# Retention and a gated feed-forward on one core: the output DMAs of seven of eight units move from SyncE's queue to GpSimd's

## The chip, the cores and the metric

The kernel runs on one core of one Trainium2 chip. The time is that of one execution on the device in microseconds (us). The engines are named as the profile names them: PE is TensorE (PEld its weight loads), DVE is VectorE, ACT is ScalarE, POOL is GpSimd, SP is SyncE; SPq and POOLq are the instruction queues of the last two, in which they issue DMAs and wait for semaphores.

## The reference

A linear attention with decay feeds a gated feed-forward with a three-tap convolution along the sequence. B, H, S, D = 4, 8, 768, 64; the model width is 512 and the inner width 1024.

```python
for t in range(S):
    state = gamma[None, :, None, None] * state + np.einsum('bhd,bhe->bhde', k[:, :, t], v[:, :, t])
    y[:, :, t] = scale * np.einsum('bhd,bhde->bhe', q[:, :, t], state)
...
h = np.maximum(x @ w_in, 0.0)
hp = np.concatenate([zeros, h, zeros], axis=1)
for k in range(K):
    conv_out += conv_w[k][None, None, :] * hp[:, k:k + S, :]
gate = 1.0 / (1.0 + np.exp(-conv_out))
return h * gate @ w_out
```

x is y with its heads side by side, so it has 4 x 768 rows of 512, and so has the result: 6.3 MB of float32.

## The kernel before

The sequence is cut into steps of 64 positions for two of the four batches: 24 steps. Each step loads q, k (both layouts) and v (L381, L385, L389, L393) into one of four `rw` buffers and makes scores, state and y (all PE work of L461, through the helper `multiply`). Three steps make a unit of 2 x 192 rows; there are eight units, 0 to 7. Of a unit, x is split into two parts of the same width by ACT (L537) and DVE (L542) and kept in one of three `xu` buffers. Then the feed-forward runs over eight pieces of the inner width: 12 matmuls of the first product into one of two PSUM banks (`ps_m`, L636), the relu by ACT which empties the bank (L643), the middle tap by ACT (L651), the outer taps by DVE (L656), and for each pair of pieces the gate by ACT (L661), its product by DVE (L666) and the split of the result by ACT and DVE (L670, L675). The second product (L688) adds up four pairs in a PSUM bank (`ps_yo`) for each tile of 128 rows, three tiles to a unit.

A finished tile is copied by ACT (`put`, L696) from PSUM into one of four staging buffers (`t2`, shared with the weights' preparation), and `out_` (L708) writes it to HBM. A unit has 192 rows of either batch, so its first and third tile are one DMA of 128 rows each, and the middle one is two of 64 rows: four DMAs for a unit. The last tile of the last unit is treated in two halves of 256 columns, which makes five DMAs for unit 7, and 33 in all.

The order of the work is written out by hand: `ORDER` has one string of letters for each of PE, DVE, ACT, POOL and the DMA queue. `plan` walks through them with estimated costs, gives every task its buffer (a staging buffer counts as free 2600 ns after its output is issued), and returns one list of tasks in the order of their estimated start. The kernel emits this list. Each engine runs its own instructions in the order of emission, and the tile framework adds the semaphore waits that the buffers need. The DMA string holds loads and outputs in one order, and both go to SP. The plan gives unit 2's three tiles one and the same staging buffer, so the copy of the second tile follows the output of the first, and that of the third the output of the second.

POOL has one kind of task, `x_tiles` (L526): a memset of the edge columns of a unit's `xu` buffer, which only units 0, 3, 4 and 7 have. In the emitted list that of unit 7 stands between the outputs of unit 2 and those of unit 3; the other three stand before the first output.

L779 is the end of the program: SP waits there for all that is open, and the engines drain and meet.

Of the kernel before, what the change touches and what calls it, by code (L numbers as in the profile page):

```python
# [18 lines left out]
P = 128  # L19
# [25 lines left out]
LAST = (len(UNITS) - 1, UNITS[-1] - 1)  # L45
# [240 lines left out]
def retention_then_gated_ffn(  # L286
# [10 lines left out]
    nc = tc.nc  # L297
# [379 lines left out]
    def columns(u, t, h):  # L677
        return slice(h * DM // 2, (h + 1) * DM // 2) if (u, t) == LAST else slice(0, DM)
# [11 lines left out]
    def put_tiles(u, t, h):  # L690
        cs = columns(u, t, h)
        return buf("t2", ("o", u, t, h))[:, : cs.stop - cs.start], buf("ps_yo", ("o", u, t, h))[:, : cs.stop - cs.start]
# [5 lines left out]
    @emits  # L698
    def out_(u, t, h):

        o, width = put_tiles(u, t, h)[0], UNITS[u] * C
        c0, tok = divmod(FIRST_STEP[u], NC)
        at = t * P
        while at < (t + 1) * P:
            b, i = divmod(at, width)
            n = min(width - i, (t + 1) * P - at)
            r0 = (c0 * G + b) * S + tok * C + i
            nc.sync.dma_start(out[r0 : r0 + n, columns(u, t, h)], o[at - t * P : at - t * P + n])  # L708
            at += n

    emit["out"] = out_
# [2 lines left out]
    for i in range(WARM_UP_SMALL):  # L714
        j, cross, at = i % 2, i // 2 % 2, i // 4 * D
# [67 lines left out]
```

## Time and profile before

| | us |
|---|---|
| runs of the kernel before | 353.55, 350.33, 352.9; median 352.9 |
| the profiled execution, its own time | 351.29 |
| its span, from the first to the last instruction | 348.9 |

PE is busy for 96% of the span, DVE for 64%, ACT for 54%, POOL for less than 1%. The granted clock of TensorE is 0.995 over the span. All DMAs that the program issues, 130 loads and 33 outputs, go through one queue; 34.0 MB are read and 6.3 MB written.

The time of a run is some 2.4 us longer than the span of the profile. Times in rows are us from the start of the span. In a timeline a row is: start, duration, engine, line, operation, written<-read tiles and shape, the count of instructions merged in the row, and in brackets the idle time of the engine before it and what ended that. For an output the profile calls the staging buffer `t` and the result `out_y`.

### The profile page before, as it was taken

How to read it: one execution, taken by the hardware profiler on the slowest of the kernel's cores; microseconds unless marked ns; L12 is line 12 of the kernel's file. 1: busy time of each engine (PE TensorE's matmuls, PEld its weight loads, DVE VectorE, ACT ScalarE, POOL GpSimd, SP SyncE). 2: the span in 40 equal slices, each digit the busy share in tenths (PEclk: the TensorE clock that was granted, in tenths of full speed). 3: DMA queues.
4: the chain of work that ended last, by engine and by line, in shares of the span. 5: the costliest groups of instructions: out<-in, count | busy, mean ns of one | idle time of the engine just before them, and what ended most of it. 6: DMA issues, size and time to landing. Idle time of an engine off the chain costs nothing.

```text
span 348.9 us, 9816 instructions
## 1 busy us (share of the span) xinstructions
PE 335.6 (96%) x4306; PEld 301.7 (86%) x4306; DVE 225.0 (64%) x370; ACT 187.4 (54%) x373; POOL 0.7 (0%) x8
## 2 busy tenths in 40 slices
PE   6879999899999999999999999999999999999996
PEld 5769999798898988988988888898889889999885
DVE  0879899979899978796666427065556242558160
ACT  1668798577675566656364345272555332545442
POOL 0000000000000000000000000000000000000000
PEclk9989999999999999999999999999999999999999
DMA  7989877958380033403003820200002001000203
GB/s 260 374 269 327 281 265 249 348 197 290 109 272 0 2 122 114 159 2 122 0 0 113 284 61 2 60 2 32 2 28 62 2 32 32 0 33 0 90 2 90
DMA packets 22491, 40.90 MB, mean 117 GB/s; under 512 B 2737, under 2 KB 2993, under 8 KB 22449
## 3 DMA queue, kind: packets, MB, share of 16 engines
q1 hardware_dynamic: 22448, 40.28, 34.4%
q8 instruction: 34, 0.56, 0.7%
q14 instruction: 9, 0.07, 0.1%
HBM read 33.98 MB, written 6.29 MB: 115 GB/s over the span
## 4 chain that ended last, share of the span: by engine, by line
PE 89%; DMA 8%; issue 1%; SPq 1%; ACT 0%
PE ps_m L636 38%; PE ps_yo L688 37%; PE ps_s L461 5%; PE ps_st L461 4%; PE ps_yo L461 4%; DMA out_y<-t 3%; DMA rw<-in_qk 3%; DMA rw<-in_kv 2%; PE ps_yo L373 1%; SPq L381 0%; ACT t L696 0%; SPq L393 0%; SPq L389 0%; SPq L385 0%; ACT hc L643 0%
## 5 line engine op out<-in xcount | busy, mean ns | idle before, releaser
L636 PE MATMUL ps_m<-xu,w 128*128 128x388 f32 x768 | 143.6, 340 | 1.0 <-ACT hc L643 1.0
L688 PE MATMUL ps_yo<-w,g 128*128 128x512 f32 (+1 forms) x600 | 140.4, 386 | 0.0
L636 PEld LDWEIGHTS ps_m<-xu,w 128*128 128x128 f32 x768 | 135.9, 188 | 4.7 <-ACT hc L643 1.4
L688 PEld LDWEIGHTS ps_yo<-w,g 128*128 128x128 f32 x600 | 108.6, 188 | 21.9
L656 DVE SCALAR_TENSOR_TENSOR hc<-hc,cw_sb,hc 128x384 f32<-128x384 f32 x128 | 74.5, 614 | 33.8 <-ACT hc L651 33.5
L643 ACT ACTIVATE hc<-ps_m 128x388 f32<-128x388 f32 x64 | 31.3, 491 | 44.5 <-PE ps_m L636 40.4
L461 PE MATMUL ps_yo<-rw 64*64 64x64 f32 (+1 forms) x1408 | 48.8, 225 | 3.1 <-issue 3.0
L461 PEld LDWEIGHTS ps_yo<-rw 64*64 64x64 f32 (+1 forms) x1408 | 45.4, 138 | 3.7 <-issue 3.3
L675 DVE TENSOR_TENSOR g<-hc,g 128x768 fp32r<-128x768 f32 x32 | 30.4, 956 | 24.6 <-ACT g L670 24.3
L666 DVE TENSOR_TENSOR hc<-hc,hc 128x768 f32<-128x768 f32 x32 | 30.3, 954 | 16.2 <-ACT hc L661 15.9
L670 ACT CAST g<-hc 128x768 fp32r<-128x768 f32 x32 | 26.5, 828 | 22.8 <-PE ps_yo L688 20.6
L651 ACT ACTIVATE hc<-hc,cw_sb 128x384 f32<-128x384 f32 x64 | 37.7, 611 | 1.4 <-DVE g L675 1.3
L661 ACT ACTIVATE hc<-hc 128x768 f32<-128x768 f32 x32 | 27.0, 846 | 16.6 <-DVE hc L656 16.5
L461 PEld LDWEIGHTS ps_s<-rw 64*64 64x64 f32 (+1 forms) x720 | 25.2, 139 | 10.4 <-issue 4.4
L461 PE MATMUL ps_s<-rw 64*64 64x64 f32 (+1 forms) x720 | 28.8, 227 | 4.0 <-DMA w<-in_w_in 2.5
L696 ACT COPY t<-ps_yo 128x512 f32<-128x512 f32 (+1 forms) x25 | 14.0, 567 | 27.0 <-PE ps_yo L688 22.3
L542 DVE TENSOR_TENSOR xu<-ps_yo,xu 128x512 fp32r<-128x512 f32 x24 | 16.5, 687 | 17.5 <-ACT xu L537 17.5
L461 PE MATMUL ps_st<-rw 64*64 64x64 f32 (+1 forms) x672 | 24.6, 222 | 0.7 <-issue 0.7
L461 PEld LDWEIGHTS ps_st<-rw 64*64 64x64 f32 (+1 forms) x672 | 22.5, 138 | 0.8 <-issue 0.8
L537 ACT CAST xu<-ps_yo 128x512 fp32r<-128x512 f32 x24 | 14.1, 592 | 13.4 <-PE ps_yo L461 12.1
L511 DVE TENSOR_TENSOR rw<-ps_s,const_sb 128x512 f32<-128x512 f32 x22 | 15.1, 686 | 8.0 <-PE ps_s L461 8.0
L519 ACT COPY rw<-ps_st 128x512 f32<-128x512 f32 x21 | 12.2, 582 | 12.8 <-PE ps_yo L461 12.7
(38 smaller groups left out, 144.4 us busy)
## 6 DMA issues: line engine op xcount, KB each, us to landing
rw<-in_qk SPq DMA_DIRECT2D x48, 256.0 KB, 4.6
rw<-in_kv SPq DMA_DIRECT2D x48, 256.0 KB, 5.1
w<-in_w_in SPq DMA_DIRECT2D x16, 256.0 KB, 5.2
w<-in_w_out SPq DMA_DIRECT2D x16, 256.0 KB, 5.0
out_y<-t SPq DMA_DIRECT2D x15, 256.0 KB, 2.2
out_y<-t SPq DMA_DIRECT2D x18, 128.0 KB, 2.4
const_sb<-in_consts SPq DMA_DIRECT2D x1, 392.0 KB, 6.2
cw_raw<-in_conv_w SPq DMA_DIRECT2D x1, 24.0 KB, 4.8
```

The lines of the kernel that those rows point to most:

```text
L461: nc.tensor.matmul(out, lhsT, rhs, start=start, stop=stop, skip_group_check=True)
L511: nc.vector.tensor_tensor(out=heads_of(n)[:, 1], in0=s_of(n), in1=mask_sb[:, :C].unsqueeze(1).unsqueeze(1).broadcast_to([P, G, NPAIR, C]), ...
L542: nc.vector.tensor_tensor(out=lo, in0=y_of(n), in1=hi.bitcast(F32), op=ALU.subtract)
L636: nc.tensor.matmul(buf("ps_m", (u, f))[:, :n], w[:, k], x[:, k], start=(i == 0), stop=(i == len(products) - 1))
L643: nc.scalar.activation(h, buf("ps_m", (u, f))[:, : G * (UNITS[u] * C + 2)], AF.Relu)
L651: nc.scalar.activation(cv, h, AF.Copy, scale=w)
L656: nc.vector.scalar_tensor_tensor(out=cv, in0=h, scalar=w, in1=cv, op0=ALU.mult, op1=ALU.add)
L661: nc.scalar.activation(cv, cv, AF.Sigmoid)
L666: nc.vector.tensor_tensor(out=cv, in0=h, in1=cv, op=ALU.mult)
L670: nc.scalar.copy(g_of(u, p)[:, 0], cv_of(u, 2 * p))
L675: nc.vector.tensor_tensor(out=lo, in0=cv_of(u, 2 * p), in1=hi.bitcast(F32), op=ALU.subtract)
L688: nc.tensor.matmul(ps, g, w[:, cs], start=(f == 0 and i == 0), stop=(f == NF - 1 and i == 2))
```

## The change

In `out_` the queue that issues the DMA depends on the unit: SP for the last unit (`LAST[0]` is 7), POOL for units 0 to 6. The strings of `ORDER`, the costs in `plan`, the buffers and the emitted list stay.

```diff
@@ -705,7 +705,7 @@
             b, i = divmod(at, width)
             n = min(width - i, (t + 1) * P - at)
             r0 = (c0 * G + b) * S + tok * C + i
-            nc.sync.dma_start(out[r0 : r0 + n, columns(u, t, h)], o[at - t * P : at - t * P + n])
+            (nc.sync if u == LAST[0] else nc.gpsimd).dma_start(out[r0 : r0 + n, columns(u, t, h)], o[at - t * P : at - t * P + n])
             at += n
```

## Rows read from the trace of the kernel before

**Rows 1.** The page, part 1: busy us, share of the span and instructions of each engine

```profile
PE 335.6 (96%) x4306; PEld 301.7 (86%) x4306; DVE 225.0 (64%) x370; ACT 187.4 (54%) x373; POOL 0.7 (0%) x8
```

**Rows 2.** Stages (from:to, length, busy us and instructions of PE, PEld, DVE, ACT, POOL; clock; DMA)

```profile
97.00:196.00 99.00, 99.00 (x1084) 87.64 (x1073) 75.59 (x122) 55.83 (x105) 0.00 (x0) 1.00 0.27 89
196.00:202.00 6.00, 4.95 (x29) 4.63 (x28) 3.74 (x7) 2.70 (x8) 0.00 (x0) 1.00 0.58 209
202.00:346.00 144.00, 143.58 (x1124) 127.69 (x1122) 67.39 (x100) 63.20 (x112) 0.13 (x1) 1.00 0.10 29
346.00:349.00 3.00, 0.00 (x0) 0.00 (x0) 0.00 (x0) 0.00 (x0) 0.00 (x0) 1.00 0.43 155
```

**Rows 3.** The line of the output DMAs, L708: issue times in ns, landing times in us

```profile
L708 SPq DMA_DIRECT2D out_y<-t x33: 332/472/1257, 136.8 to 346.0; - x33
...
DMA to landing us min/median/max: 1.8/2.3/5.8
```

**Rows 4.** Waits of PE after 97 us: total, times, longest

```profile
PE ps_m L636 <- ACT hc L643: 1.0, 1, 1.0
```

**Rows 5.** Waits of ACT after 97 us: total, times, longest

```profile
ACT t L696 <- DMA out_y<-t: 4.5, 2, 3.3
```

**Rows 6.** Timeline of all engines, 195 to 208 us

```profile
195.88 4.42 PE L636 MATMUL ps_m<-xu,w 128*128 128x388 f32 x24
...
196.42 0.59 ACT L537 CAST xu<-ps_yo 128x512 fp32r<-128x512 f32 x1
...
200.31 0.59 ACT L696 COPY t<-ps_yo 128x512 f32<-128x512 f32 x1 [3.30 <-DMA out_y<-t]
200.79 0.50 ACT L643 ACTIVATE hc<-ps_m 128x388 f32<-128x388 f32 x1
200.92 3.92 SPq L708 DMA_DIRECT2D out_y<-t  x3
...
201.35 4.54 PE L636 MATMUL ps_m<-xu,w 128*128 128x388 f32 x24 [1.05 <-ACT hc L643]
...
201.83 0.62 DVE L656 SCALAR_TENSOR_TENSOR hc<-hc,cw_sb,hc 128x384 f32<-128x384 f32 x1 [1.83 <-ACT hc L651]
...
203.24 1.14 DVE L656 SCALAR_TENSOR_TENSOR hc<-hc,cw_sb,hc 128x384 f32<-128x384 f32 x2
203.88 0.59 ACT L696 COPY t<-ps_yo 128x512 f32<-128x512 f32 x1 [1.20 <-DMA out_y<-t]
204.37 0.62 ACT L651 ACTIVATE hc<-hc,cw_sb 128x384 f32<-128x384 f32 x1
...
205.93 0.49 ACT L643 ACTIVATE hc<-ps_m 128x388 f32<-128x388 f32 x1 [0.56 <-PE ps_m L636]
206.10 0.13 POOL L526 MEMSET xu<- 128x16 f32 x1 [121.96 <-PE ps_m L636]
...
207.12 1.05 PE L636 MATMUL ps_m<-xu,w 128*128 128x388 f32 x5
```

**Rows 7.** Timeline of SP's queue, 122 to 207 us

```profile
187.62 0.34 SPq L381 DMA_DIRECT2D rw<-in_qk  x1
...
188.96 1.11 SPq L708 DMA_DIRECT2D out_y<-t  x2
...
194.45 0.43 SPq L708 DMA_DIRECT2D out_y<-t  x1
```

**Rows 8.** Timeline of ACT, 150 to 200 us

```profile
158.63 0.57 ACT L696 COPY t<-ps_yo 128x512 f32<-128x512 f32 x1
...
185.89 0.57 ACT L696 COPY t<-ps_yo 128x512 f32<-128x512 f32 x1
```

**Rows 9.** Timeline of ACT, 228 to 290 us

```profile
285.73 0.60 ACT L537 CAST xu<-ps_yo 128x512 fp32r<-128x512 f32 x1
```

**Rows 10.** The end of the program, L779: durations in ns min/median/max, first and last start

```profile
L779 SPq EVENT_SEMAPHORE  x7: 17/28/1489, 346.4 to 348.9; - x7
...
L779 POOLq DRAIN  x3: 34/78/204, 206.1 to 348.7; - x3
```

## The prediction

> **What bounds the kernel now.** I read the page's busy table first: PE is busy 335.6 us of a span of 348.9, DVE 225.0, ACT 187.4, and POOL 0.7 [rows 1]. The table of stages then says where PE's remaining time is. From 97 to 196 us it does not pause at all (99.00 of 99.00), from 196 to 202 it lacks 1.05 us, from 202 to 346 it lacks 0.42, and the last 3 us are the outputs of the last tile [rows 2]. The first output is issued at 136.8 us [rows 3], so nothing before 97 us can be touched by this change, and all that can be won before the tail is 1.05 + 0.42 = 1.47 us. PE's list of waits after 97 us has one line: 1.0 us, for a result of L643 on ACT [rows 4]. ACT's list has the line behind it: the copy L696 waited twice, 4.5 us in all, for an output DMA, the longest time 3.3 us [rows 5].
>
> The timeline shows how these two are one event [rows 6]. ACT ends its L537 at 196.42 + 0.59 = 197.01. Its next instruction is the copy of unit 2's second tile into the staging buffer out of which the first tile is still being written. It stands until 200.31, 3.30 us, released by that DMA. Behind it in ACT's order is the L643 that frees the PSUM bank which PE's next L636 writes; it starts at 200.79, ends near 201.3, and PE, through with 24 matmuls at 195.88 + 4.42 = 200.30, starts again at 201.35. That is the 1.05 us.
>
> Why was the DMA late? The first tile had been copied by 185.89 + 0.57 = 186.46 [rows 8], but the output was issued only at 194.45 [rows 7]. SP runs its queue in order, and a load stood there until 187.62 for its buffer; more loads and unit 1's late outputs came before it. The same queue held the outputs of unit 1's second tile, copied by 158.63 + 0.57 = 159.20 [rows 8], until 188.96, some 30 us, with no one waiting for them.
>
> **The change part by part.** *Removed from SP:* 28 of 33 issues (seven units of four; the last unit keeps five), median 0.47 us each [rows 3], 13.2 us. SP has long idle times and PE waits for no load after 97 us [rows 4], so I take nothing for this. The loads after 187.62 can leave sooner by the two issues at 188.96 (1.11 us) and some more [rows 7]; no cover is needed, since nothing waits.
>
> *Added to POOL:* the same 28. No row shows a POOL output, so its cost d, the time for which it holds POOL's queue before its bytes go, is bounded by what stands nearest: below by a POOL memset, 0.13 us [rows 6], above by SP's slowest issue, 1.26 us, and for the worst by the 5.8 us that the slowest output took to land [rows 3]. I take 1.26 us, the upper of the two issue times, as no row speaks for a POOL quicker than SP's slowest. The Trainium skill (DMA: Bandwidth & Descriptors, "Latency and other measured facts") gives about 1 us to the first byte from GpSimd against 0.6 from Sync; with that price, an estimate of 0.4 us more for each output, the sum below stays as it is.
>
> *POOL's order.* It holds the memset of L526 for unit 7 between the outputs of unit 2 and unit 3. The memset ran at 206.10, as PE released its tile [rows 6], and ACT's next write of that kind of tile for unit 7 is the L537 at 285.73 [rows 9]. Unit 2's last output, issued near 202 to 205, delays it by at most a few us of the 80 that are free. The memsets of units 0, 3 and 4 stand before every output in the emitted order, and of unit 3's outputs, behind the fourth, none is due before PE has passed that point. So the queue costs nothing.
>
> *Moved: unit 2's outputs.* The first is issued when its copy ends, at 186.46, its bytes leave by 187.7, and even with the slowest landing, 5.8 us, it is down at 193.5. The copy of the second tile needs it at 197.01. So that copy runs from 197.01 to 197.60, its L643 runs once PE has finished the first 12 matmuls of the 24 (195.88 + 2.21 = 198.09), and PE finds its bank free at 200.30. Gain 1.05 us.
>
> *What is late next.* The third copy uses the same staging buffer, so it waits for the second tile's two outputs of 64 rows. These are issued after 197.60; with 2 x 1.26 for POOL and the median landing of 2.3 us [rows 3] they are down at 202.4. The limit: PE's next but one L636 set began at 207.12 and would begin at 206.07. Before it ACT must do the copy, L651, and two L643 (a step of 0.49 us each, as from 203.88 to 204.37 [rows 6], 2.0 in all, and some 0.05 to PE, as from 200.79 + 0.50 to 201.35), so the third copy must start by 204.0. It has 1.6 us to spare, or in terms of d: 197.60 + 2d + 2.3 = 204.0 gives d = 2.05 us. No other copy waits for an output now [rows 5].
>
> *The end.* The last unit's outputs, with the last 3 us, are as before. SP's closing waits get more members: it has 7 now at a median of 28 ns, POOL's drains take 34 to 204 ns [rows 10]. Bounds: nothing, and 28 waits of 28 ns with 28 drains of 34 ns, 1.7 us. I take as many waits again as now, 7 x 0.028 = 0.2 us.
>
> Sum against the profiled execution's own time, 351.29 us (a span of 348.9 and 2.4 around it): 351.29 - 1.05 + 0.2 = **350.4 us**, a gain of 0.85. The median of the runs shown, 352.9, stands 1.6 above this execution; from it the same gain gives 352.05. I name the middle, **351.2 us**. About 1% is what a measurement of this kernel tells from no change (its runs reach from 350.33 to 353.55), so the forecast is "no change that can be told", with PE's pause gone.
>
> **The rivals.** *1. The pause only moves.* If d is near 2.3 us, the third copy is late by half a microsecond, and at 2.6 by 1.05: the gain is used up and the closing waits remain: 351.0 to 351.5 by the profiled execution. For it: no row prices a POOL output. Against: 1.6 us to spare.
>
> *2. Slower: POOL's outputs come one behind the other.* The place is the third copy of unit 2. From d = 2.6 us the copy holds L643, and so PE, longer than today. At d = 4 us the second tile is down at 197.60 + 8 + 2.3 = 207.9, 3.9 us beyond the limit: 351.29 - 1.05 + 3.9 + 0.2 = 354.3. For it: a DMA in this trace has taken 5.8 us. Against: the one waited for until 200.31 was issued at 194.45 amid loads [rows 7]; the outputs after it landed within 203.88 - 200.92 = 2.96 us, two issues included [rows 6].
>
> *3. POOL can work only while DVE rests.* DVE rests for 1.83 us up to 201.83, and then works nearly without a break through 204.4 (203.24 + 1.14) [rows 6]. If an output's preparation must fall into such a rest and the rest takes both, they are down near 200.0 + 2.96 = 203.0, in time. But that rest ends with an L651 of ACT which the change makes earlier, so it may shrink to one output; then the second goes at 204.4, is down at 206.7, and PE stands 2.7 us: 351.29 - 1.05 + 2.7 + 0.2 = 353.1. Against: nothing in the rows ties POOL to DVE; the memset at 206.10 ran as soon as PE released its tile [rows 6]. The Trainium skill (SBUF — State Buffer, "SBUF: two separate sides") has such a rule: GpSimd cannot write its descriptors while DVE runs an operation in a mode that takes both ports, and it tells of a DMA that went from about 620 to 3100 ns. It names that mode and not every DVE operation, and no run here shows the mode; the case above is what it would make of this place.
>
> *4. POOL holds up DVE.* The place is unit 6's four outputs after its copies, where unit 7's last products are made. With all of 4 x 1.26 = 5.0 us taken from DVE and no slack at PE: 351.29 - 1.05 + 5.0 + 0.2 = 355.4. Against: DVE works 67.39 of the last 144 us [rows 2].
>
> *5. The outputs are no sooner*, because they wait for something else than SP's order: 351.5. Against: the 8.0 us from 186.46 to 194.45 are filled by SP's rows alone.
>
> **How the numbers follow.** Forecast 0.62, rival 1 0.13, rival 2 0.10, rival 3 0.06, rival 4 0.04, rival 5 0.05. The low end: the lowest run, 350.33, less about 1.05; the largest possible gain of 1.47 would bring it to 348.9. The high end: rival 2 at 354.3, which leaves out rival 4 and the scatter above it. Range 349.3 to 354.3. Faster by over 1% (3.5 us) cannot come from a pool of 1.47 us, only from scatter: 0.03. Slower by over 1% needs 354.8: rival 4 and the long part of rival 2, 0.08. Within 1%: 0.89.
>
> **What would show it.** In the profile after: the copy L696 waits for no output DMA between 187 and 205; PE's waits after 97 us lose the line of L643, and PE from 196 to 202 is busy 6.0 of 6.0; the chain no longer runs through output DMAs near 190; unit 1's outputs are issued within 2 us of their copies. The third copy of unit 2 starts before 204. The prediction is wrong if a POOL output holds its queue over 2 us, if the pause stands at the same place or a new one appears within 10 us behind it, if DVE's L656 gets longer than its 0.62 us [rows 6] beside outputs, or if the end after the last matmul grows by over 1 us.

## The result, and the profile after

The changed kernel takes 349.14 us (median of 20 runs, 347.90 to 351.26), the kernel before 353.19 us beside it (20 runs, 350.33 to 357.01). The ratio is 0.9901, with an interval from 0.9877 to 0.9925: a gain of 0.0099 x 353.19 = 3.5 us, between 2.6 and 4.3. (The ratio leaves out runs over 1.5% above the fastest of their kernel, which is why it stands nearer to 1 than 349.14 / 353.19 = 0.9885.) The direction held. The size did not, as 0.85 us was forecast, nor did "no change that can be told", as the interval leaves out 1. Of the range, 349.3 to 354.3, the result stands at the low end: the median is 0.16 us below it, and the ratio taken of the median that the prediction had, 0.9901 x 352.9 = 349.4, just inside. The change also drew the runs together, from 6.7 us between the extremes to 3.4.

The profiled execution took 349.01 us, its span 346.8. First its page, which answers to [rows 1]; the third line is a DMA queue that was not there before (packets, MB, share of 16 DMA engines), the fourth the line of DVE that was feared for (count, total us and mean ns).

```profile
span 346.8 us, 9822 instructions
...
PE 334.7 (97%) x4306; PEld 300.9 (87%) x4306; DVE 224.8 (65%) x370; ACT 187.6 (54%) x373; POOL 16.2 (5%) x36
...
q0 software_dynamic: 1792, 5.51, 5.1%
...
L656 DVE SCALAR_TENSOR_TENSOR hc<-hc,cw_sb,hc 128x384 f32<-128x384 f32 x128 | 74.5, 614 | 32.3 <-ACT hc L651 32.0
```

POOL's 15.5 us more are the 28 outputs; DVE's total has not grown. Of its stages, the one in which PE paused before, with the columns of [rows 2]:

```profile
196.00:202.00 6.00, 6.00 (x36) 6.00 (x35) 5.46 (x9) 4.05 (x9) 1.66 (x3) 1.00 0.21 50
```

PE fills it, 6.00 of 6.00 against 4.95. Its list of waits after 97 us, which had the one line of [rows 4], is empty. In ACT's list the copy no longer waits for an output DMA, as it did in [rows 5], only for PE:

```profile
ACT t L696 <- PE ps_yo L688: 22.3, 9, 5.3
```

The timeline around the old pause shows the whole chain of [rows 6]:

```profile
195.03 8.65 PE L636 MATMUL ps_m<-xu,w 128*128 128x388 f32 x48
...
196.06 0.58 ACT L696 COPY t<-ps_yo 128x512 f32<-128x512 f32 x1
...
196.81 0.61 DVE L656 SCALAR_TENSOR_TENSOR hc<-hc,cw_sb,hc 128x384 f32<-128x384 f32 x1
196.94 1.08 POOL L708 DMA_DIRECT2D out_y<-t  x2 [10.78 <-ACT t L696]
197.34 0.69 DVE L430 TENSOR_TENSOR rw<-rw,const_sb 128x512 f32<-128x512 f32 x1
...
200.38 0.58 ACT L696 COPY t<-ps_yo 128x512 f32<-128x512 f32 x1
...
201.25 0.58 POOL L708 DMA_DIRECT2D out_y<-t  x1 [3.23 <-DVE hc L656]
...
203.80 0.12 POOL L526 MEMSET xu<- 128x16 f32 x1 [1.97 <-issue]
```

The second copy starts at 196.06 and the third at 200.38, both without a wait, and the 24 + 24 matmuls with the pause between them are one row of 48. Unit 2's first output left right behind its copy (185.61, with the copy ended at 184.74 + 0.57 = 185.31), and unit 1's three later outputs at 158.34, not near 189:

```profile
158.34 1.80 POOL L708 DMA_DIRECT2D out_y<-t  x3 [2.08 <-ACT t L696]
185.61 0.55 POOL L708 DMA_DIRECT2D out_y<-t  x1 [25.47 <-ACT xu L563]
```

What one output costs POOL's queue, and how it lands, is in the rows of L708, with the columns of [rows 3] (the wait events of POOL and SP are left out):

```profile
L708 POOL DMA_DIRECT2D out_y<-t x28: 538/548/681, 129.3 to 327.5; - x28
...
L708 SPq DMA_DIRECT2D out_y<-t x5: 332/409/586, 341.2 to 343.8; - x5
...
DMA to landing us min/median/max: 1.9/2.3/5.8
```

The end, with the columns of [rows 10], has four more waits on SP. One of POOL's three drains takes 3.54 us now, where the longest took 0.20, but from the end of the last matmul to the end of the span it is 3.4 us against 3.3.

```profile
L779 SPq EVENT_SEMAPHORE  x11: 17/28/28, 344.2 to 346.7; - x11
...
L779 POOLq DRAIN  x3: 40/102/3542, 327.4 to 346.4; - x3
```

The two profiled executions are 351.29 - 349.01 = 2.28 us apart. It splits at the start of the 24 matmuls ahead of the pause: 195.88 before, 195.03 after, which is 0.85 us; from there to PE's last matmul 149.70 before, 148.33 after, 1.37 us; the rest is 0.06. Of the 1.37, the pause is 1.05, and 0.31 is that the 48 matmuls around it took 4.42 + 4.54 = 8.96 us in two rows before and 8.65 in one row after. That leaves two questions: whether the 0.85 us of the loading stage belong to the change, and why the medians differ by 3.5 to 4 us when this pause and what hangs on it came to 1.4.

### The profile page after: what moved, and what is told of

It reads as the page before. It is cut to its first block, busy times and chain, and to the rows that moved or that the text cites. A ratio compares the mean times of both kernels' runs of the same rounds, so it can differ in the third digit from the quotient of the medians.

```text
span 346.8 us, 9822 instructions
## 1 busy us (share of the span) xinstructions
PE 334.7 (97%) x4306; PEld 300.9 (87%) x4306; DVE 224.8 (65%) x370; ACT 187.6 (54%) x373; POOL 16.2 (5%) x36
## 4 chain that ended last, share of the span: by engine, by line
PE 92%; DMA 3%; SPq 2%; issue 2%; ACT 0%
PE ps_m L636 40%; PE ps_yo L688 39%; PE ps_s L461 5%; PE ps_yo L461 4%; PE ps_st L461 4%; DMA rw<-in_kv 2%; DMA rw<-in_qk 1%; SPq L581 1%; PE ps_yo L373 1%; SPq L381 0%; SPq L385 0%; SPq L389 0%; SPq L393 0%; SPq L397 0%; ACT t L696 0%
## 5 line engine op out<-in xcount | busy, mean ns | idle before, releaser
L656 DVE SCALAR_TENSOR_TENSOR hc<-hc,cw_sb,hc 128x384 f32<-128x384 f32 x128 | 74.5, 614 | 32.3 <-ACT hc L651 32.0
L461 PE MATMUL ps_yo<-rw 64*64 64x64 f32 (+1 forms) x1408 | 47.6, 221 | 1.9 <-issue 1.9
L461 PEld LDWEIGHTS ps_yo<-rw 64*64 64x64 f32 (+1 forms) x1408 | 44.0, 135 | 3.8 <-issue 3.4
L461 PEld LDWEIGHTS ps_s<-rw 64*64 64x64 f32 (+1 forms) x720 | 24.4, 136 | 9.9 <-issue 5.0
L461 PE MATMUL ps_s<-rw 64*64 64x64 f32 (+1 forms) x720 | 28.0, 223 | 3.7 <-DMA w<-in_w_in 1.7
L708 POOL DMA_DIRECT2D out_y<-t x28 | 15.5, 557 | 227.8 <-ACT t L696 199.0
L696 ACT COPY t<-ps_yo 128x512 f32<-128x512 f32 (+1 forms) x25 | 13.9, 566 | 22.5 <-PE ps_yo L688 22.3
```

The costliest lines, as they stand in the source:

```text
L461: nc.tensor.matmul(out, lhsT, rhs, start=start, stop=stop, skip_group_check=True)
L656: nc.vector.scalar_tensor_tensor(out=cv, in0=h, scalar=w, in1=cv, op0=ALU.mult, op1=ALU.add)
L708: (nc.sync if u == LAST[0] else nc.gpsimd).dma_start(out[r0 : r0 + n, columns(u, t, h)], o[at - t * P : at - t * P + n])
```

## The experiments

Two theories answer the second. Theory A: the pause is all that the change removes, and in the one profiled execution it happened to be short; in most it is longer and costs more. Theory B: something in the queues themselves is won, SP being rid of 28 issues or the DMAs of POOL being better, and the pause is only the smaller part. A says that anything which removes the pause gains the full amount, also with every output on SP, and that moving other outputs gains nothing.

**Only unit 2's outputs on POOL; only unit 6's; and, all on SP, the outputs ahead of the loads.** The first two replace the choice of the queue; the third moves three letters in the hand-written order of SP, and no output is on POOL.

```diff
-nc.sync.dma_start(...)
+(nc.gpsimd if u == 2 else nc.sync).dma_start(...)   (e2)
+(nc.gpsimd if u == 6 else nc.sync).dma_start(...)   (e3)
-        "vqkqtktqvvotovktqkooqkvovoqktttovoooooooooooooooooo"
+        "vqkqtktqvvotovktqkoooooqkvvqktttvoooooooooooooooooo"   (e1)
```

> Only unit 2's four outputs go by GpSimd, the other 29 by SyncE. Theory A: the pause is gone, ratio 0.988 to 0.993. Theory B: the pause of 1.05 us is gone and a small part of the rest, ratio 0.995 to 0.997. If the second and third copy of unit 2 stop waiting for outputs, but PE still pauses, both are wrong.

> Only unit 6's four outputs go by GpSimd. Theory A: the pause stays and its profile gives another sample of its length, 1 to 8 us, ratio 0.998 to 1.002. Theory B: the pause stays, about 1 us, and GpSimd's queue is in use, ratio 0.992 to 0.997.

> All outputs stay on SyncE; only the order of SyncE's queue changes: unit 1's last two outputs and unit 2's first output stand ahead of the ten loads that they followed. Theory A (the gain is the pause of PE at unit 2's second copy, and in an ordinary run the pause is longer than the 1.05 us of the one profiled execution, some 3 us in the median): no pause, no wait of the copy L696 for an output, ratio 0.988 to 0.993, as with GpSimd's queue. Theory B (the pause is 1.05 us, and some 2.5 us come from GpSimd's queue itself, for instance from a shorter SyncE queue): no pause, ratio 0.996 to 0.998. Theory C (the loading phase before 97 us got quicker): PE busy over 0 to 97 us as before, 88.1, and ratio 0.996 to 0.998.

All three ran beside the kernel before at 353.77 us. Unit 2 alone: 349.15 us, ratio 0.9882 [0.9835, 0.9930]. Unit 6 alone: 354.73 us, 0.9990 [0.9946, 1.0034]. SP's order alone: 348.32 us, 0.9874 [0.9820, 0.9928]. Within these intervals four outputs of 28 carry the whole gain, four others none, and without POOL the gain is the same (0.9874 lies just below the 0.988 that theory A allowed). In the SP kernel's timeline the output follows its copy by 0.02 us, and the second copy waits for nothing:

```profile
184.01 0.57 ACT L696 COPY t<-ps_yo 128x512 f32<-128x512 f32 x1
...
195.01 0.59 ACT L696 COPY t<-ps_yo 128x512 f32<-128x512 f32 x1
```

```profile
184.60 0.34 SPq L708 DMA_DIRECT2D out_y<-t  x1
```

Theory B falls.

The Trainium skill (Perfetto Trace Analysis, "DMA Optimizations") suggests giving inputs one issuing engine and outputs another; the runs agree that it helps here, and show that the order within one queue does the same.

**The late output kept, the shared buffer removed.** The plan chooses, among free staging buffers, the one with the lowest number; here, for outputs, it chooses the one free for longest. The queues and the hand-written orders are as before.

```diff
-            i = min(some, key=lambda i: (max(some[i], t), i))
+            i = min(some, key=lambda i: (max(some[i], t), some[i] if name == "t2" and owner[0] == "o" else 0, i))
```

> All outputs stay on SyncE in the old order; a tile takes the staging buffer that has been free the longest, so unit 2's three tiles have three buffers. The outputs are as late as before, but no copy of unit 2 waits for one. Theory A: ratio 0.988 to 0.993, though SyncE's queue is unchanged. Theory B: 0.996 to 0.998.

It took 348.85 us, ratio 0.9878 [0.9829, 0.9926], the whole gain again (and again just below 0.988). Unit 2's first output is as late as ever, issued at 194.14, 8.5 us after its copy (185.09 + 0.57 = 185.66), but the second copy, at 196.16, does not care:

```profile
194.14 1.52 SPq L708 DMA_DIRECT2D out_y<-t  x1
```

```profile
196.16 0.59 ACT L696 COPY t<-ps_yo 128x512 f32<-128x512 f32 x1
```

So the late output costs nothing here by itself. The cost is the copy that waits for it, and PE behind that copy.

**How long the pause is in other executions.** The unchanged kernel once more, and one with only unit 4's outputs on POOL (its edit is that of e2 with 4), which leaves unit 2 as it was.

> The kernel before, unchanged, as one more sample of the pause. Theory A: PE's pause behind L643 differs from the 1.05 us of the first profile, within 0.5 to 8 us, and ends with the landing of unit 2's first output; the loads beside that output take a different time. Theory B: 1.0 to 1.1 us again.

> Only unit 4's four outputs go by GpSimd, so that the pause at unit 2 stays; a further sample of its length, 0.5 to 8 us by theory A and 1.0 to 1.1 by theory B, and its own time less the pause between 347.5 and 351.5 us.

They took 351.65 and 352.83 us, one run each, beside a single run of before at 353.33. The unchanged kernel's second profile has the same chain, with other lengths:

```profile
194.28 4.42 PE L636 MATMUL ps_m<-xu,w 128*128 128x388 f32 x24
...
199.65 0.58 ACT L696 COPY t<-ps_yo 128x512 f32<-128x512 f32 x1 [4.25 <-DMA out_y<-t]
...
200.69 6.07 PE L636 MATMUL ps_m<-xu,w 128*128 128x388 f32 x24 [1.99 <-ACT hc L643]
```

The pause is 1.99 us where it was 1.05 in [rows 6], and the 24 matmuls behind it take 6.07 us instead of 4.54. The windows of two microseconds behind the pause, with the columns of [rows 2], show why:

```profile
202.00:204.00 2.00, 2.00 (x8) 2.00 (x7) 1.72 (x3) 0.80 (x3) 0.00 (x0) 0.50 0.29 68
204.00:206.00 2.00, 2.00 (x10) 2.00 (x9) 0.00 (x0) 0.70 (x2) 0.00 (x0) 0.68 0.37 135
```

The granted clock is 0.50 there, the lower of the two levels (1.2 GHz), and PE gets 8 matmuls into two microseconds. In the profile of before the same two microseconds hold 13, at 1.00:

```profile
202.00:204.00 2.00, 2.00 (x13) 2.00 (x12) 2.00 (x4) 0.80 (x3) 0.00 (x0) 1.00 0.56 131
```

With unit 4 alone moved, the pause is 2.47 us and 24 matmuls again take 6.07; in the profile of unit 6 alone they are 3.52 and 6.06:

```profile
202.03 6.07 PE L636 MATMUL ps_m<-xu,w 128*128 128x388 f32 x24 [2.47 <-ACT hc L643]
```

```profile
205.59 6.06 PE L636 MATMUL ps_m<-xu,w 128*128 128x388 f32 x24 [3.52 <-ACT hc L643]
```

What varies is how long the output stands behind loads. For the four profiles in which unit 2's first output is on SP and shares its buffer with the next, from the rows of L696 and L708 (us):

| | first copy ends | its output issued | second copy starts | issued after copy | second copy after first | less 12.80 | pause seen |
|---|---|---|---|---|---|---|---|
| before | 186.46 | 194.45 | 200.31 | 7.99 | 13.85 | 1.05 | 1.05 |
| before again | 184.85 | 194.31 | 199.65 | 9.46 | 14.80 | 2.00 | 1.99 |
| unit 4 alone | 185.73 | 195.67 | 200.99 | 9.94 | 15.26 | 2.46 | 2.47 |
| unit 6 alone | 188.23 | 199.10 | 204.55 | 10.87 | 16.32 | 3.52 | 3.52 |

The 12.80 is the slack, that is, how long after the first copy the second may start without holding up PE; it is fitted in the first line, and it gives the other three within 0.01 us. The output's way from issue to the second copy is much the same, 5.3 to 5.9 us; the wait for issue spans 2.9 us. SP's rows place it in the loads. In all four profiles the first load leaves 1.2 us after the copy's end, and the outputs between take 1.54 us; but the rows of loads ahead of unit 2's output take 4.4, 6.2, 6.7 and 7.6 us together. The third load alone takes 0.44 us in the profile of before and 2.27 in that of unit 6 alone:

```profile
188.48 0.44 SPq L393 DMA_DIRECT2D rw<-in_kv  x1
```

```profile
190.26 2.27 SPq L393 DMA_DIRECT2D rw<-in_kv  x1
...
199.10 0.43 SPq L708 DMA_DIRECT2D out_y<-t  x1
```

```profile
204.55 0.58 ACT L696 COPY t<-ps_yo 128x512 f32<-128x512 f32 x1 [5.77 <-DMA out_y<-t]
```

Why a load's issue stands longer in some executions was not tried. The four profiles also come from more than one chip (the record has chip 0 for before again and unit 4 alone, 4 for unit 6 alone), so what belongs to the chip and what to the execution is not told apart.

**A pause of chosen length, with all outputs early.** On top of the change, POOL copies unit 2's second tile onto itself n times ahead of its outputs (n = 2, 8, then 4 and 5; a single run of each). This holds POOL's queue for a time that the trace shows, and so delays the third copy, which shares the buffer.

```diff
+        for _ in range(n * ((u, t) == (2, 1))):
+            nc.gpsimd.tensor_copy(o, o)
```

> The changed kernel, with GpSimd held before the outputs of unit 2's second tile: it copies the staged tile onto itself twice after ScalarE's copy (the result stays the same). Let h be GpSimd's time from its first such copy to the end of the last. In the changed kernel's trace these outputs were issued by 198.02 us, land some 2 us later, and the third copy may start as late as 204.91 - 2.05 = 202.86 without a pause of PE. So PE's pause is h - 2.9 us, or none: at two copies (h some 1 to 2.2 us) none. If the third copy has no slack: a pause of h.

> The same with eight copies, h some 4 to 9 us. With the limit as worked out: the third copy waits for the output, and PE pauses once, behind L643, for h - 2.9 us within 0.5. If the third copy has no slack: h. If it is not on the path at all: no pause. Were GpSimd's work to hold up VectorE, L656 would be longer than 0.62 us beside these copies.

> The changed kernel with four copies on GpSimd before the outputs of unit 2's second tile. Eight copies took 7.46 us and two 1.50, so h is 3.73; PE's pause is 3.73 - 2.9 = 0.8 us, within 0.3. The longer pauses seen so far (2.0 us and more) were followed by a stretch with a granted clock of 0.50, the one of 1.05 us was not. Theory A2 (a pause of this size costs itself alone): granted clock 1.00 after it, the next 12 matmuls of L636 take their 2.3 us, the cost is 0.8 to 1.0 us. Theory A3 (any pause at this place costs the clock too): 0.50 for some us, the 12 matmuls take 3 us or more, cost 2.5.

> The same with five copies, h 4.66 us: PE's pause is 1.8 us, within 0.3. A2 and A3 both allow the fall of the clock here, as after the pause of 2.0 us; if it falls, the cost is 1.8 + 1.7 = 3.5 us, if not, 1.8 to 2.0.

The prediction's limit was that the third copy must start by 204.0, 8.12 us after the start of the 24 matmuls at 195.88. Against that (us; times are those of one profile each):

| copies | POOL held | third copy, from the start of the 24 | less 8.12 | pause seen | whole time |
|---|---|---|---|---|---|
| 2 | 1.50 | 201.62 - 194.99 = 6.63 | none | none | 348.93 |
| 4 | 3.40 | 203.70 - 195.18 = 8.52 | 0.40 | 0.39 | 349.70 |
| 5 | 4.42 | 207.32 - 197.78 = 9.54 | 1.42 | 1.40 | 353.45 |
| 8 | 7.46 | 206.21 - 193.63 = 12.58 | 4.46 | 4.45 | 353.87 |

The pause sets in where the limit says. With four and five copies it is shorter than expected (0.8 and 1.8, within 0.3), by 0.4 each: they held POOL less than their share of the eight (3.73 and 4.66), and what POOL can be held without a pause is 3.0 us and not the 2.9 of the expectations (3.40 - 0.39, 4.42 - 1.40, 7.46 - 4.45). The high time with five is the loading stage: its 24 matmuls start at 197.78, 2.6 us later than with four.

The clock again tells the long pause from the short. Behind 1.40 us PE goes on at 1.00, with 13 matmuls in two microseconds; behind 4.45 us it has 0.50 and 7. First five copies, then eight, with the third copy of the latter:

```profile
209.24 2.40 PE L636 MATMUL ps_m<-xu,w 128*128 128x388 f32 x12 [1.40 <-ACT hc L643]
```

```profile
210.00:212.00 2.00, 2.00 (x13) 1.90 (x12) 0.00 (x0) 0.33 (x1) 0.00 (x0) 1.00 0.01 2
```

```profile
193.63 8.66 PE L636 MATMUL ps_m<-xu,w 128*128 128x388 f32 x48
...
208.13 3.67 PE L636 MATMUL ps_m<-xu,w 128*128 128x388 f32 x12 [4.45 <-ACT hc L643]
```

```profile
206.21 0.58 ACT L696 COPY t<-ps_yo 128x512 f32<-128x512 f32 x1 [7.12 <-DMA out_y<-t]
```

```profile
210.00:212.00 2.00, 2.00 (x7) 1.94 (x6) 0.00 (x0) 0.16 (x1) 0.00 (x0) 0.50 0.00 0
```

**What a pause costs in all.** Each profile can be cut as the first two were: the start of the 24 matmuls, and the time from there to the end of PE's last row. The seven profiles without a pause (the changed kernel twice, unit 2 alone, SP's order, the buffers, two copies, and the last kernel below) have 148.33 to 148.36 us for the second part. What the others have above 148.35 is the price of their pause:

| | start of the 24 | to PE's end | above 148.35 | pause |
|---|---|---|---|---|
| 4 copies | 195.18 | 149.02 | 0.67 | 0.39 |
| before | 195.88 | 149.70 | 1.35 | 1.05 |
| 5 copies | 197.78 | 150.05 | 1.70 | 1.40 |
| before again | 194.28 | 152.17 | 3.82 | 1.99 |
| unit 4 alone | 195.14 | 152.67 | 4.32 | 2.47 |
| unit 6 alone | 197.65 | 153.70 | 5.35 | 3.52 |
| 8 copies | 193.63 | 154.63 | 6.28 | 4.45 |

Up to 1.40 us a pause costs itself and 0.3; from 1.99 us on, itself and 1.8. The four executions that have the old pause lost 1.35, 3.82, 4.32 and 5.35 us: 4.1 in the middle, 3.7 on average, close to the measured gain (3.5 by the ratio, 4.05 by the medians). Four executions are few, and that of unit 6 alone was a long one (356.35 us); without it the average is 3.2. The record has a hint from more runs, their mean granted clock: of the 17 runs of the kernel before that stood beside the first four experiments, the six from 350.33 to 352.50 us have 0.995, the eleven from 353.43 us up 0.984 to 0.990, and of the 20 runs of the changed kernel only three have 0.990 or less. The profile of before has 0.995, the three with the longer pause 0.989. It is no more than a hint, as such a mean does not tell the place (the kernel with eight copies has 0.995).

The 0.85 us of the loading stage are answered too. The start of the 24 lies anywhere from 193.60 to 197.78 in the fourteen profiles, with eight copies near the low end (193.63) and with five at the high one. In each of them PE is busy for over 95 of the 96 us from 97 to 193, and no output is issued before 128.2. So that start is set in the loading stage, before there is any output to move, and no output's queue can have made the 0.85 us.

**Both repairs on SP, beside the changed kernel.** SP's order of e1 and the buffers of e4, no output on POOL; and the changed kernel again.

> All outputs on SyncE with the order of e1 and the buffers of e4 together. Theory A: nothing is left to gain at this place, ratio 0.985 to 0.993, within 0.5 us of the changed kernel of this call; the end after the last matmul 0.1 us shorter, as GpSimd's semaphores are not waited for. Theory B: slower than the changed kernel by 2 us or more.

> The changed kernel beside e11: ratio 0.988 to 0.993, no pause of PE after 97 us.

The first took 347.52 us, ratio 0.9853 [0.9810, 0.9896], the second 349.92 us, ratio 0.9929 [0.9895, 0.9964], the kernel before being at 353.65. They were expected within 0.5 us of each other; the medians are 2.4 apart, and the intervals touch at 0.9895. Neither profile has a pause of PE after 97 us, and both have 148.35 us from the start of the 24 to PE's end; they differ by 1.90 us in that start (193.60 and 195.50), within the scatter just shown. The SP version is at least as good, and whether it is better stays open.

## Why the prediction was right, and where it was wrong

**The pause goes: right in place and mechanism.** The second copy waited for an output that stood behind loads in SP's queue; the output leaves at 185.61 now, the copy runs at 196.06, PE does not stop. Moving that output by another way, or giving the copy another buffer, does the same; moving unit 6's outputs alone gains nothing, and with unit 4's alone the pause stays.

**"Gain 1.05 us": the step that failed.** The term of the sum was mis-sized: the pause was worth 1.35, 3.82, 4.32 and 5.35 us in four executions, and the profile that the prediction read showed the smallest. Two things were missing. First, the 1.05 was taken as a property of the kernel, though it is a difference: the time from the first copy to the second (13.85 us, and up to 16.32 elsewhere, of which the output stands 8.0 to 10.9 in a queue among loads) less a slack of 12.80 that does not vary. A small rest between two long times moves by as much as the longer one scatters. The prediction saw the median 1.6 us above the profiled execution and took that for scatter without a place, though a longer pause was a place for it. Second, behind a longer pause the granted clock fell to 0.50, which added 1.5 us; the profile of before, at 1.00 from 97 us on [rows 2], had no row of that.

**"Faster by over 1% cannot come from a pool of 1.47 us": wrong by the same step.** The gain, 0.99% with an interval from 0.75 to 1.23, lies on that bound. The pool was one execution's. That the range reached as low as the result was luck: its low end was the lowest run less 1.05, so the scatter of the runs brought it there, and not the size of the gain.

**POOL's hold of 1.26 us an output: too high.** It is 0.55 (538 to 681 ns), near SP's median of 0.47. The argument did not hang on it: the limit of 2.05 us stood far above either. The limit for the third copy was exact: counted from it, the runs with copies on POOL gave the pauses within 0.02 us.

**POOL's order costs nothing: right.** The memset for unit 7 ran at 203.80, with no one behind it.

**The end, +0.2 us: 0.1 by the span.** SP has 11 waits instead of 7, and still a median of 28 ns.

**The rivals.** *The pause only moves* and *slower, outputs one behind the other*: the third copy had no wait in the changed kernel and 0.88 us with unit 2 alone on POOL, where the start at 201.59 is 6.34 us after that of the 24 at 195.25, within 8.12. A late third copy does stop PE, as the runs with copies on POOL show, but POOL has to be held 3.0 us longer than the outputs hold it. *POOL works only while DVE rests*: the two outputs at 196.94 took 1.08 us across two DVE instructions; how outputs fare beside the mode of DVE that the prediction names, no run shows. *POOL holds up DVE*: L656 is 614 ns in the mean, and 0.61 right beside outputs. *No sooner*: 0.30 us after the copy, not 7.99.

## What to carry to other kernels

A small stall in a trace is a difference of two long times: before taking it for what a change can win, write it as "arrival less slack", see how much the arrival can scatter (here a queue in which an output stands behind loads), and compare the profiled execution with the median. Behind one in-order queue of loads and stores, a store whose buffer is wanted soon goes ahead of the loads that can wait, or the next tile gets another buffer; a second queue is one way of three that gave the same. Price a pause of PE by the matmuls behind it too, since a change that shortens one may win back a granted clock that the profile at hand does not show as lost (here 1.5 us).

## What the runs showed of the hardware that was not expected

PE's granted clock fell to 0.50 behind pauses of 1.99, 2.47, 3.52 and 4.45 us and stayed at 1.00 behind those of 0.39, 1.05 and 1.40; PE had been busy nearly without a break for some 90 us before each (over 95 of the 96 us from 97 to 193 in each; in the profile of before, wholly). At 0.50 it did 7 or 8 matmuls in two microseconds instead of 13.

POOL's own copies, unlike its outputs, make DVE slower. Beside the eight copies of the 8-copy kernel:

```profile
196.25 1.09 DVE L430 TENSOR_TENSOR rw<-rw,const_sb 128x512 f32<-128x512 f32 x1
197.27 0.96 DVE L656 SCALAR_TENSOR_TENSOR hc<-hc,cw_sb,hc 128x384 f32<-128x384 f32 x1
```

```profile
195.31 7.46 POOL L704 COPY t<-t 128x512 f32<-128x512 f32 x8 [10.24 <-ACT t L696]
```

L656 takes 0.96 us where it took 0.61 beside outputs (the row at 196.81 of the changed kernel), L430 1.09 where it took 0.69. The Trainium skill (SBUF — State Buffer, "Who interferes with whom") has such a rule: a DVE instruction with two inputs from SBUF contends with a GpSimd instruction that reads SBUF. The rows agree as to DVE; how long a copy of POOL takes with DVE at rest no run shows. The start of the third copy alone gives PE's pause in that kernel within 0.01 us, so the slower DVE seems to have cost nothing there.
